# Fused attention and gated MLP on one core: one decoded weight part, two operands and the last product are placed elsewhere

## The chip, the cores and the metric

The kernel runs on one core of one Trainium2 chip. The metric is the device time of one execution in microseconds (us); lower is better. The engines that matter are PE (TensorE, matrix products), DVE (VectorE), ACT (ScalarE), POOL (GpSimd, adds only here) and SP (SyncE), whose queue issues nearly all DMAs in order.

## The reference

Inputs are float32, 8 batches, 12 heads, 448 positions, head size 64. The MLP weights have 768 x 2048 and 2048 x 768 elements and come as float64 words, which the kernel decodes itself.

```python
scores = scale * np.matmul(q, k.transpose(0, 1, 3, 2)) - np.log(S)
attn = 1.0 / (1.0 + np.exp(-scores))
x = np.matmul(attn, v)            # then (batch, position, 768)
h = x @ w_in
g = h * np.clip(h + 3.0, 0.0, 6.0) / 6.0
out = g @ w_out
```

## The kernel before, in words

**Numbers.** Each operand of the MLP is split into a high and a low part of type fp32r, and a product takes three passes (high x high, high x low, low x high). An operand therefore costs a cast on ACT or DVE and a subtraction on DVE ("put", L238 to L242, for x; `split_w`, L271, for weights; `split_2`, L394, for the second layer).

**Seven products instead of eight.** Both MLP layers are cut into 2 x 2 blocks and use a seven-product scheme; the products are called P1, P5, P6, P2, P7, P3, P4 in the order in which they run. For x the four blocks are two batches by two halves of the heads; the sums of blocks are made by `minus` and `put`. P7 and P3 use the blocks b12 and b22 ("late" in `t_ops`, L259).

**Stages.** There are four runs of attention, over batches (0,1,2,3), (4), (5,6) and (7), called runs 0 to 3, and after each a first-layer product for one pair of batches, called products 0 to 3 (`quads`). The names carry the number n. After product 3 come four blocks of the second layer (`block`, n = 0 to 3), and then the program ends. The "third pair" of batches is n = 2: its attention is run 2 (batches 5 and 6; batch 4 was done in run 1) and its product is product 2. The last single-batch run is run 3.

**A first-layer product** has four rounds jj = 0 to 3. A round makes two hidden parts i = 0, 1, and each of its 7 x 2 products has 9 matmuls, so a round has 126 matmuls and a product stage 504. Within a round, the accumulator z[P1] collects P1, P6, P7 and P4. `seed2` (L321, DVE) reads z[P1] into another bank before P7 may add to it, so **P7 waits for L321**. `h22` (L325, DVE, tile snh) reads z[P1] before P4 may add to it. Both sit in DVE's queue among the splits of weights (L275), the gates (L338), the differences (L343) and whatever else is put there.

**Decoded parts.** `prep` (L101 to L161) decodes one of eight parts of a weight matrix. A part has two halves u = 0, 1. Each half has one load (L108, SP), one ACT operation (L118), five DVE operations (L123, L125, L127, L131, L133, called "a set" below) and one POOL add (L137). Then come four POOL sums (L146) and seven stores to DRAM (L151, SP). The eight parts of w_out are placed from run 0's end to product 2; the last three, j = 5, 6, 7, all lie in product 2.

**The second layer.** For each n and each product k, eight units u of 9 matmuls: three output chunks e (banks y, y, yb) by three passes. `split_2` makes weights and g for two units at a time, with four buffers each, so all eight units of one product fit exactly. `keep`, `middle` and `out` (L422 to L446) empty the banks; `out` on P4 is an ACT multiplication (L443) and a store per chunk.

**What sets the order.** The whole program is a list of pairs (place, function). `at(place, f)` adds one; the list is sorted by place, an estimated time in us, and is emitted in that order on PE, ACT, DVE and POOL. SP's order is worked out separately from estimated readiness. An instruction waits only for data and for the one ahead of it on its engine, so a place decides who stands behind whom. In the places, TU is 1.863 us (nine matmuls), `marks[n]` is the start of product n, `starts[n]` that of run n, and `free` is the end of product n - 1.

Of the kernel before, what the change touches and what calls it, by code (L numbers as in the profile page):

```python
# [17 lines left out]
P = 128  # L18
# [5 lines left out]
NT = B // 2  # L24
# [19 lines left out]
def tile_kernel(ctx: ExitStack, tc: tile.TileContext, qk, vP, w8, outT):  # L44
# [358 lines left out]
    def block(n, place):  # L403
        z, sn = {}, {}

        def unit(k, u):
            if u == 0:
                if k in (P6, P7, P4):
                    z[k] = z[P1]
                else:  # L410
                    t = pair_banks(f"y_{n}_{k}", n + (k != P1))
                    z[k] = [t[:, 0], t[:, 1], bank(f"yb_{n}_{k}", 2 * (n % 2) + (k != P1))]
            w, x = ring.pop((n, k, u)), x2.pop((n, k, u))
            for e in range(HC):
                for i, (wu, xu) in enumerate(passes):
                    nc.tensor.matmul(  # L416
                        z[k][e][:, :S], w[:, wu, e * P : (e + 1) * P], x[:, xu],
                        start=u == 0 and i == 0 and k in (P1, P5, P2, P3), stop=u == HF - 1 and i == 2,
                        skip_group_check=True,
                    )  # L420

        def keep(k):  # L422
            for e in range(HC):
                t = two["b"].tile([P, S], F32, tag=f"sn{k}{e}", name=f"sn2_{n}_{k}_{e}")
                nc.scalar.mul(t, z[k][e][:, :S], sixth)
                sn[k, e] = t

        def plus(dst, k, e, s):
            nc.vector.scalar_tensor_tensor(
                out=dst, in0=z[k][e][:, :S], scalar=sixth, in1=sn[s, e], op0=ALU.mult, op1=ALU.add  # L430
            )

        def middle():
            for e in range(HC):
                t = two["b"].tile([P, S], F32, tag=f"c12{e}", name=f"c12_{n}_{e}")
                plus(t, P6, e, P5)
                sn["c12", e] = t

        def out(k, s, eh, th):
            for e in range(HC):  # L440
                o = two["b"].tile([P, S], F32, tag="o", name=f"o_{n}_{k}_{e}", bufs=4)
                if s is None:
                    nc.scalar.mul(o, z[k][e][:, :S], sixth)  # L443
                else:
                    plus(o, k, e, s)
                nc.sync.dma_start(out=outT[2 * n + th, e + eh * HC], in_=o)  # L446

        d = HF * TU
        for k in range(NW):
            at(place + k * d - 26, load_g, n, k)  # L450
            if n == 0:
                at(place + k * d - 24, load_w2, k)
            for u in range(HF):
                at(place + k * d + u * TU, unit, k, u)
                if u % 2 == 0:
                    at(place + k * d + u * TU - 6 * TU + 0.3, split_2, n, k, u)
        e = 0.3
        at(place + 1 * d + e, keep, P1)
        at(place + 2 * d + e, keep, P5)
        at(place + 3 * d + e, middle)  # L460
        at(place + 4 * d + e, out, P2, P1, 0, 0)
        at(place + 5 * d + e, out, P7, P5, 1, 1)
        at(place + 6 * d + e, out, P3, "c12", 0, 1)
        at(place + 7 * d + e, out, P4, None, 1, 0)

# [32 lines left out]
    for c in range(HC):  # L500
        for n in range(NT):
            own = [taken[2 * n + (h % 2), c + HC * (h // 2)] for h in range(4)]
            free = marks[n - 1] + HF * q if n else 0.0
            start = marks[n]
            if n == 0:
                early = ((own[0], dve), (own[2], dve))
                upper, both, gap = (max(own[1], own[0] + 1.2), dve), own[3] + 0.1, 1.4
                late = ((own[3] + 11, dve), (own[3] + 12.5, dve))
            elif n == 1:
                early = ((free - 11.6 * TU + 2.2 * c, act), (free - 0.5 + 9 * c, dve))  # L510
                upper, both, gap = (free - 9.6 * TU + 3 * c, act), free + 0.7 + 9 * c, 1.2
                late = ((start - 5 + 1.3 * c, dve), (start + 2 * TU + 1.5 * c, act))
            else:
                early = ((free - 11.6 * TU + 2.2 * c, act), (free - 5.6 * TU + 2.2 * c, act))
                upper, both, gap = (own[1] + 0.1, dve), own[3] + 0.1, 1.2 if n < 3 or c < 2 else 0.1
                if n == 2:
                    late = ((start - 30 + 10 * c, dve), (start - 25 + 10 * c, dve))
                else:
                    late = ((start + 4 * TU + 1.5 * c, act), (start + 6 * TU + 1.5 * c, act))
            t_ops(n, c, early, upper, both, late, gap)  # L520
    for j in range(HF):
        prep(0, j, (8, 26, 44, 74, 92, 110, 128, 146)[j], 9)
    for j, place in enumerate((
        marks[0] + 40, marks[1] + 18, marks[1] + 50, starts[2] + 26, starts[2] + 45, marks[2] + 14, marks[2] + 42, marks[2] + 68
    )):
        prep(1, j, place, 12)
    at(marks[3] + 6, open_two)
    at(now + 5.5, close_one)
    first = now
    at(now - 0.01, open_four, "psy")  # L530
# [55 lines left out]
```

## Time and profile before

| | us |
|---|---|
| three timed runs | 1118.78, 1115.82, 1117.30 (median 1117.30) |
| the profiled execution's own time | 1117.07 |
| its span, first to last instruction | 1115.2 |
| outside the span | 1.87 |
| mean granted PE clock | 0.992 |

A row of the timeline gives the start and the length in us, the engine, the line, the operation, output and input tiles, and the number of instructions merged into the row; in brackets stands how long the engine sat idle before it and who released it. Matmuls overlap: their spacing is the length of a merged row divided by its count, not the length of one. The busy length of a DVE row also overlaps the next one a little, so costs are read from start to start.

### The profile page before, as it was taken

What the parts mean: (1) busy time and instruction counts of PE and PEld (TensorE: products, weight loads), DVE (VectorE), ACT (ScalarE), POOL (GpSimd) and SP (SyncE); (2) the same over time, 40 slices, a digit from 0 to 9 for tenths busy, and PEclk for the clock granted to TensorE, in tenths of its full rate; (3) what the DMA queues carried; (4) which work ended last, traced back from release to release, by engine and by line L of the source; (5) the groups of instructions that cost most, each with busy time, mean ns of one, the idle gap of its engine ahead of it and who ended that gap; (6) DMA issues with size and microseconds to landing.
All of it is one profiled execution on the core that took longest, in us unless ns stands there. A gap on an engine that the chain in (4) does not pass through costs nothing.

```text
span 1115.2 us, 17907 instructions
## 1 busy us (share of the span) xinstructions
PE 1087.1 (97%) x6720; PEld 880.5 (79%) x6720; DVE 816.8 (73%) x1101; ACT 622.2 (56%) x841; POOL 149.1 (13%) x102
## 2 busy tenths in 40 slices
PE   8999998999999999999899999999999999999998
PEld 3447697974998743898756889999999999999997
DVE  4898799997699869799958577766655655665663
ACT  7878845457554678544467354554554455445542
POOL 1524533200033003233300000000000000000000
PEclk9999999999999999999899999999999999999999
DMA  7997998965598746899743984674533553454341
GB/s 248 294 327 231 332 336 277 338 243 169 167 318 294 278 135 211 299 309 316 243 163 99 379 301 162 263 332 157 199 132 133 182 182 132 134 173 175 110 143 60
DMA packets 95271, 250.23 MB, mean 224 GB/s; under 512 B 10576, under 2 KB 66256, under 8 KB 90704
## 3 DMA queue, kind: packets, MB, share of 16 engines
q1 hardware_dynamic: 95040, 249.01, 64.9%
q8 instruction: 53, 0.87, 0.3%
q14 instruction: 34, 0.28, 0.1%
q10 hardware_dynamic: 144, 0.07, 0.0%
HBM read 164.63 MB, written 84.41 MB: 223 GB/s over the span
## 4 chain that ended last, share of the span: by engine, by line
PE 73%; DVE 10%; DMA 8%; issue 5%; POOL 2%; ACT 2%; SPq 0%; ACTq 0%; DVEq 0%; POOLq 0%
PE y L416 24%; PE z L305 20%; PE yb L416 12%; PE sc L198 7%; PE pv L224 7%; DMA raw<-wd 2%; DVE w L275 2%; DMA gr<-gd 2%; POOL ws L146 1%; PE sc L193 1%; DVE t L343 1%; DMA st<-wi 1%; PE pv L218 1%; DVE g L338 1%; POOL wa L137 1%
## 5 line engine op out<-in xcount | busy, mean ns | idle before, releaser
L305 PE MATMUL z<-x,w 128*128 128x448 f32 x2016 | 420.5, 371 | 14.8 <-DVE z L321 12.8
L305 PEld LDWEIGHTS z<-x,w 128*128 128x128 f32 x2016 | 383.7, 191 | 52.9 <-issue 11.4
L416 PE MATMUL y<-x,w 128*128 128x448 f32 x1344 | 307.9, 364 | 0.0
L416 PEld LDWEIGHTS y<-x,w 128*128 128x128 f32 x1344 | 252.0, 187 | 19.9
L275 DVE TENSOR_TENSOR w<-w,w 128x768 fp32r<-128x768 f32 x112 | 107.3, 958 | 147.4 <-ACT w L274 146.3
L204 ACT ACTIVATE a<-sc,bias_s 128x896 f32<-128x896 f32 x168 | 168.4, 1009 | 52.4 <-PE sc L198 37.1
L274 ACT CAST w<-w 128x768 fp32r<-128x768 f32 x112 | 93.8, 838 | 184.6 <-PE yb L416 180.9
L416 PE MATMUL yb<-x,w 128*128 128x448 f32 x672 | 171.9, 364 | 0.0
L275 DVE TENSOR_TENSOR w<-raw,w 128x768 fp32r<-128x768 f32 x112 | 124.8, 1116 | 43.9 <-ACT w L274 40.2
L198 PE MATMUL sc<-qk 64*64 64x448 f32 x1152 | 149.5, 544 | 5.5 <-DMA qk<-qk 3.7
L224 PE MATMUL pv<-a,v 64*64 64x448 f32 x1152 | 149.6, 537 | 3.5 <-DVE xr L233 1.3
L416 PEld LDWEIGHTS yb<-x,w 128*128 128x128 f32 x672 | 126.0, 187 | 9.9
L399 DVE TENSOR_TENSOR x<-gr,x 128x896 fp32r<-128x896 f32 x112 | 121.6, 1086 | 6.5 <-ACT x L398 6.5
L137 POOL TENSOR_TENSOR wa<-wa,st 128x768 f32<-128x768 f32 x32 | 64.6, 2017 | 403.2 <-DVE st L133 328.7
L274 ACT CAST w<-raw 128x768 fp32r<-128x768 f32 x112 | 93.2, 832 | 38.3 <-PE z L305 17.0
L398 ACT CAST x<-gr 128x896 fp32r<-128x896 f32 x112 | 104.9, 937 | 6.5 <-DMA gr<-gd 6.5
L198 PEld LDWEIGHTS sc<-qk 64*64 64x64 f32 x1152 | 53.5, 134 | 66.0 <-issue 43.4
L224 PEld LDWEIGHTS pv<-a,v 64*64 64x64 f32 x1152 | 54.3, 133 | 61.7 <-issue 47.2
L335 ACT ACTIVATE g<-z,bias 128x448 f32<-128x448 f32 x96 | 59.8, 633 | 75.9 <-PE z L305 43.0
L335 ACT ACTIVATE g<-snh,bias 128x448 f32<-128x448 f32 x32 | 21.5, 671 | 78.1 <-DVE snh L325 75.1
L338 DVE SCALAR_TENSOR_TENSOR g<-g,z 128x448 f32<-128x448 f32 x96 | 58.4, 613 | 6.6 <-ACT g L335 6.6
L241 DVE TENSOR_TENSOR x<-xr,x 128x448 fp32r<-128x448 f32 x84 | 56.8, 678 | 8.5 <-ACT x L240 6.4
(43 smaller groups left out, 679.0 us busy)
## 6 DMA issues: line engine op xcount, KB each, us to landing
gr<-gd SPq DMA_DIRECT2D x28, 1792.0 KB, 8.2
raw<-wd SPq DMA_DIRECT2D x112, 384.0 KB, 4.8
gd<-t SPq DMA_DIRECT2D x128, 224.0 KB, 4.0
gd<-g SPq DMA_DIRECT2D x96, 224.0 KB, 3.9
qk<-qk SPq DMA_DIRECT2D x47, 448.0 KB, 5.7
st<-wi SPq DMA_DIRECT2D x16, 768.0 KB, 5.5
wd<-ws SPq DMA_DIRECT2D x64, 192.0 KB, 5.2
st<-wo SPq DMA_DIRECT2D x16, 768.0 KB, 5.6
```

The costliest lines, as they stand in the source:

```text
L137: nc.gpsimd.tensor_tensor(out=a, in0=a, in1=e, op=ALU.add)
L198: nc.tensor.matmul(sc[halves[h], j, :S], k[halves[j], ks], q[halves[j]], start=True, stop=True)
L204: nc.scalar.activation(a, sc[:, :, :S], AF.Sigmoid, bias=bias_s, scale=scale)
L224: nc.tensor.matmul(pv[b, hp][h][halves[j], :S], v[halves[h], j * NC + c], a[halves[h], j], start=c == 0 and not (second and shared), stop= ...
L274: nc.scalar.copy(h, src)
L275: nc.vector.tensor_tensor(out=l, in0=src, in1=h.bitcast(F32), op=ALU.subtract)
L305: nc.tensor.matmul(z[i, k][:, :S], w[:, wu, c * P : (c + 1) * P], X[n, k, c][:, xu], start=m == 0 and k in (P1, P5), stop=m == 3 * HC - 1, ...
L335: nc.scalar.activation(new(i, o), src(i, o), AF.Relu, bias=bias_3, scale=1.0)
L338: nc.vector.scalar_tensor_tensor(out=g[i, o], in0=g[i, o], scalar=6.0, in1=src(i, o), op0=ALU.min, op1=ALU.mult)
L398: nc.scalar.copy(x[:, 0], src)
L399: nc.vector.tensor_tensor(out=x[:, 1], in0=src, in1=x[:, 0].bitcast(F32), op=ALU.subtract)
L416: nc.tensor.matmul(z[k][e][:, :S], w[:, wu, e * P : (e + 1) * P], x[:, xu], start=u == 0 and i == 0 and k in (P1, P5, P2, P3), stop=u == H ...
```

## The change

1. **Last decoded part.** The eighth part of w_out (j = 7) moves from `marks[2] + 68`, in product 2, to `starts[3] + 1`, in run 3. The parts j = 5 and 6 stay in product 2, but move from +14 and +42 to +20 and +56. The pool of the attention (`open_two` closes it) is released at `marks[3] + 20` instead of + 6.
2. **Third pair's last two operands.** The operands of P7 and P3 of n = 2 were made before product 2, in run 2, with the casts on DVE. They are now made inside product 2 with the casts on ACT, as those of n = 3 already were.
3. **Last partial product.** The last P4 (n = 3) ran unit by unit, each over the three output chunks. It now runs chunk by chunk (`column`), each over the eight units, and each chunk is emptied when it is done.
4. In the second layer the last split of each product is placed 1 us earlier.

```diff
+        def column(k, e):
+            if e == 0:
+                z[k] = z[P1]
+            for u in range(HF):
+                w, x = ring[n, k, u], x2[n, k, u]
+                for i, (wu, xu) in enumerate(passes):
+                    nc.tensor.matmul(
+                        z[k][e][:, :S], w[:, wu, e * P : (e + 1) * P], x[:, xu],
+                        start=False, stop=u == HF - 1 and i == 2, skip_group_check=True,
+                    )
...
-        def out(k, s, eh, th):
-            for e in range(HC):
+        def out(k, s, eh, th, es=range(HC)):
+            for e in es:
...
-                at(place + k * d + u * TU, unit, k, u)
+                if (n, k) != (NT - 1, P4):
+                    at(place + k * d + u * TU, unit, k, u)
                 if u % 2 == 0:
-                    at(place + k * d + u * TU - 6 * TU + 0.3, split_2, n, k, u)
+                    at(place + k * d + u * TU - 6 * TU + 0.3 - (u == HF - 2), split_2, n, k, u)
...
-        at(place + 7 * d + e, out, P4, None, 1, 0)
+        if n < NT - 1:
+            at(place + 7 * d + e, out, P4, None, 1, 0)
+        else:
+            for h in range(HC):
+                at(place + (6 + h / HC) * d + 0.01, column, P4, h)
+                at(place + (6 + (h + 1) / HC) * d + e, out, P4, None, 1, 0, (h,))
...
-                if n == 2:
-                    late = ((start - 30 + 10 * c, dve), (start - 25 + 10 * c, dve))
-                else:
-                    late = ((start + 4 * TU + 1.5 * c, act), (start + 6 * TU + 1.5 * c, act))
+                late = ((start + 4 * TU + 1.5 * c, act), (start + 6 * TU + 1.5 * c, act))
...
-        marks[0] + 40, marks[1] + 18, marks[1] + 50, starts[2] + 26, starts[2] + 45, marks[2] + 14, marks[2] + 42, marks[2] + 68
+        marks[0] + 40, marks[1] + 18, marks[1] + 50, starts[2] + 26, starts[2] + 45, marks[2] + 20, marks[2] + 56, starts[3] + 1
...
-    at(marks[3] + 6, open_two)
+    at(marks[3] + 20, open_two)
```

**First place: DVE in the last round of product 2, ahead of the seed that its P7 waits for.** `wa_7` and `st_7_1` are the second half of part j = 7, `w_6_4` and `w_6_5` are weight splits, `x_0_0` to `x_0_2` are subtractions for the next pair, and `z_3_5_0` is the seed. Before:

```order
L343 TENSOR_TENSOR t_2_2_1_5461<-g_2_2_1_5449,t_2_2_1_5429 128x448
L123 TENSOR_SCALAR wa_7_5324<-wa_7_5324 128x768
L125 TENSOR_SCALAR wa_7_5324<-wa_7_5324 128x768
L241 TENSOR_TENSOR x_0_0_5491<-xr_0_4386,x_0_0_5491 128x448
L275 TENSOR_TENSOR w_6_4_5494<-raw_3_4_5365,w_6_4_5494 128x768
L127 SCALAR_TENSOR_TENSOR wa_7_5324<-st_7_1_5363,wa_7_5324 128x768
L241 TENSOR_TENSOR x_0_1_5510<-xr_1_4513,x_0_1_5510 128x448
L131 TENSOR_SCALAR st_7_1_5363<-wa_7_5324 128x768
L133 SCALAR_TENSOR_TENSOR st_7_1_5363<-st_7_1_5363 128x768
L275 TENSOR_TENSOR w_6_5_5526<-raw_3_5_5405,w_6_5_5526 128x768
L241 TENSOR_TENSOR x_0_2_5529<-xr_2_4629,x_0_2_5529 128x448
L321 TENSOR_TENSOR z_3_5_0_5541<-z_3_0_0_5439,sne_3_0_5508 128x448
```

After the change, the same place on DVE:

```order
L343 TENSOR_TENSOR t_2_2_1_5442<-g_2_2_1_5425,t_2_2_1_5405 128x448
L241 TENSOR_TENSOR x_0_0_5472<-xr_0_4380,x_0_0_5472 128x448
L275 TENSOR_TENSOR w_6_4_5475<-raw_3_4_5341,w_6_4_5475 128x768
L241 TENSOR_TENSOR x_0_1_5490<-xr_1_4501,x_0_1_5490 128x448
L275 TENSOR_TENSOR w_6_5_5508<-raw_3_5_5381,w_6_5_5508 128x768
L241 TENSOR_TENSOR x_0_2_5511<-xr_2_4611,x_0_2_5511 128x448
L321 TENSOR_TENSOR z_3_5_0_5523<-z_3_0_0_5415,sne_3_0_5488 128x448
```

The five decode operations ahead of this seed are gone. From the second round's seed to the third's, ten decode operations stood before and seven stand now; from the third's to the fourth's, ten before and six now.

**Second place: DVE at the start of run 3.** `xr_0` is the first attention result that is taken from its bank, `x_1_0` the operand made from it. Before, the take follows the last difference of product 2 directly:

```order
L343 TENSOR_TENSOR t_2_3_1_5731<-g_2_3_1_5711,t_2_3_1_5692 128x448
L233 TENSOR_TENSOR xr_0_5787<-pv_0_1_5740,xr_0_5787 128x448
L245 TENSOR_TENSOR xr_0_4386<-xr_0_5787,xr_0_4386 128x448
L240 CAST x_1_0_5806<-xr_0_4386 128x448
L241 TENSOR_TENSOR x_1_0_5806<-xr_0_4386,x_1_0_5806 128x448
L233 TENSOR_TENSOR xr_3_5833<-pv_3_1_5779,xr_3_5833 128x448
```

After, on DVE at the same place:

```order
L343 TENSOR_TENSOR t_2_3_1_5704<-g_2_3_1_5682,t_2_3_1_5663 128x448
L123 TENSOR_SCALAR wa_7_5693<-wa_7_5693 128x768
L125 TENSOR_SCALAR wa_7_5693<-wa_7_5693 128x768
L127 SCALAR_TENSOR_TENSOR wa_7_5693<-st_7_0_5592,wa_7_5693 128x768
L131 TENSOR_SCALAR st_7_0_5592<-wa_7_5693 128x768
L133 SCALAR_TENSOR_TENSOR st_7_0_5592<-st_7_0_5592 128x768
L233 TENSOR_TENSOR xr_0_5767<-pv_0_1_5714,xr_0_5767 128x448
L245 TENSOR_TENSOR xr_0_4380<-xr_0_5767,xr_0_4380 128x448
L240 CAST x_1_0_5787<-xr_0_4380 128x448
L241 TENSOR_TENSOR x_1_0_5787<-xr_0_4380,x_1_0_5787 128x448
L233 TENSOR_TENSOR xr_3_5814<-pv_3_1_5758,xr_3_5814 128x448
L123 TENSOR_SCALAR wa_7_5693<-wa_7_5693 128x768
```

The first half's set stands ahead of the first take; the second half's set is spread over the operations from the second take to the third.

**Third place: PE in the last product of the program.** `x_3_6_0` to `x_3_6_6` and `w_6_0` to `w_6_6` are g and weights, two units to a tile. Before, the last rows are:

```order
L416 MATMUL y_0_9273<-x_3_6_4_9900,w_6_4_9897 128x448 x6
L416 MATMUL yb_0_9274<-x_3_6_4_9900,w_6_4_9897 128x448 x3
L416 MATMUL y_0_9273<-x_3_6_6_9924,w_6_6_9921 128x448 x6
L416 MATMUL yb_0_9274<-x_3_6_6_9924,w_6_6_9921 128x448 x3
L416 MATMUL y_0_9273<-x_3_6_6_9924,w_6_6_9921 128x448 x6
L416 MATMUL yb_0_9274<-x_3_6_6_9924,w_6_6_9921 128x448 x3
```

After, PE's last ten rows are:

```order
L428 MATMUL y_0_9279<-x_3_6_4_9900,w_6_4_9897 128x448 x6
L428 MATMUL y_0_9279<-x_3_6_6_9915,w_6_6_9912 128x448 x6
L428 MATMUL y_0_9279<-x_3_6_0_9852,w_6_0_9849 128x448 x6
L428 MATMUL y_0_9279<-x_3_6_2_9876,w_6_2_9873 128x448 x6
L428 MATMUL y_0_9279<-x_3_6_4_9900,w_6_4_9897 128x448 x6
L428 MATMUL y_0_9279<-x_3_6_6_9915,w_6_6_9912 128x448 x6
L428 MATMUL yb_0_9280<-x_3_6_0_9852,w_6_0_9849 128x448 x6
L428 MATMUL yb_0_9280<-x_3_6_2_9876,w_6_2_9873 128x448 x6
L428 MATMUL yb_0_9280<-x_3_6_4_9900,w_6_4_9897 128x448 x6
L428 MATMUL yb_0_9280<-x_3_6_6_9915,w_6_6_9912 128x448 x6
```

The last tile of weights and g, `w_6_6` and `x_3_6_6`, is now needed after 18 matmuls instead of after 54, and only the chunk yb is still open when PE ends.

## The prediction

> **What bounds the kernel now.** First the page: busy time, and the slices of the span.
>
> ```profile
> span 1115.2 us, 17907 instructions
> PE 1087.1 (97%) x6720; PEld 880.5 (79%) x6720; DVE 816.8 (73%) x1101; ACT 622.2 (56%) x841; POOL 149.1 (13%) x102
> ...
> DVE  4898799997699869799958577766655655665663
> ...
> PEclk9999999999999999999899999999999999999999
> ```
>
> PE is busy for 97% of the span, so an edit can only win what PE waits (some 28 us) and what it computes at a reduced clock. The PEclk row has one 8, in slice 20 (530 to 558 us), and DVE is at 9 there. Next, who PE waits for, and the two stages that the change touches.
>
> ```profile
> PE z L305 <- DVE z L321: 12.8, 5, 4.7
> ...
> 449.60:564.70 115.10, 108.39 (x508) 97.87 (x505) 103.25 (x139) 53.64 (x85) 37.36 (x23) 0.96 0.84 284
> 565.00:597.50 32.50, 31.88 (x336) 12.35 (x328) 19.96 (x36) 25.33 (x30) 0.00 (x0) 1.00 0.36 118
> ```
>
> The largest wait is for the seed L321, 12.8 us in five waits. Product 2 (449.6 to 564.7) has DVE busy for 103.25 of 115.1 us and a clock of 0.96; run 3 has DVE busy for 19.96 of 32.5 and POOL idle. So DVE is the bound in product 2, and has room in run 3. PE's timeline gives the single losses.
>
> ```profile
> 276.87 65.94 PE L305 MATMUL z<-x,w 128*128 128x448 f32 x324
> ...
> 440.74 0.60 PE L224 MATMUL pv<-a,v 64*64 64x448 f32 x3 [1.06 <-DVE xr L233]
> ...
> 518.96 27.34 PE L305 MATMUL z<-x,w 128*128 128x448 f32 x126 [1.97 <-DVE z L321]
> 551.01 13.76 PE L305 MATMUL z<-x,w 128*128 128x448 f32 x54 [4.72 <-DVE z L321]
> 564.70 1.74 PE L198 MATMUL sc<-qk 64*64 64x448 f32 x16
> ...
> 640.01 7.53 PE L305 MATMUL z<-x,w 128*128 128x448 f32 x36 [2.10 <-DVE z L321]
> ```
>
> Undisturbed, product 1 runs at 65.94 / 324 = 0.2035 us a matmul. After the stall of 1.97 us, 126 matmuls took 27.34 instead of 25.64: 1.70 lost. After that of 4.72, 54 took 13.69 (to 564.70) instead of 10.99: 2.70 lost. After 2.10 us at 640, 36 took 7.53 against 7.33: nothing. The windows say what the loss is (the third number from the end is the granted clock).
>
> ```profile
> 519.00:522.00 3.00, 3.00 (x9) 2.65 (x10) 3.00 (x5) 0.65 (x1) 2.84 (x3) 0.51 0.94 298
> ...
> 552.00:555.00 3.00, 3.00 (x10) 2.69 (x9) 3.00 (x5) 0.00 (x0) 3.00 (x3) 0.50 0.52 112
> ```
>
> A stall can thus cost its own length and then about 1.7 us at half clock. Product 2 loses 1.97 + 1.70 + 4.72 + 2.70 = **11.1 us**.
>
> [...] Without the 1.7 the sum below would be 1107.2.
>
> **The seeds of product 2, counted on DVE.** Here are the seeds of rounds 1, 2 and 3, one decode set between them, and what POOL does to DVE.
>
> ```profile
> 489.11 1.16 DVE L321 TENSOR_TENSOR z<-z,sne 128x448 f32<-128x448 f32 x2
> ...
> 504.40 2.29 DVE L343 TENSOR_TENSOR t<-g,g 128x448 f32<-128x448 f32 x1
> ...
> 512.86 0.55 DVE L123 TENSOR_SCALAR wa<-wa 128x768 f32<-128x768 f32 x1
> 513.45 0.56 DVE L125 TENSOR_SCALAR wa<-wa 128x768 int32<-128x768 int32 x1
> ...
> 514.79 0.95 DVE L127 SCALAR_TENSOR_TENSOR wa<-st,wa 128x768 int32<-128x768 int32 x1
> 515.85 0.56 DVE L131 TENSOR_SCALAR st<-wa 128x768 int32<-128x768 int32 x1
> 516.44 0.96 DVE L133 SCALAR_TENSOR_TENSOR st<-st 128x768 f32<-128x768 uint32 x1
> ...
> 518.19 1.15 DVE L321 TENSOR_TENSOR z<-z,sne 128x448 f32<-128x448 f32 x2
> 519.25 1.54 DVE L275 TENSOR_TENSOR w<-raw,w 128x768 fp32r<-128x768 f32 x1
> ...
> 521.78 1.78 DVE L275 TENSOR_TENSOR w<-raw,w 128x768 fp32r<-128x768 f32 x1
> 523.48 1.37 DVE L123 TENSOR_SCALAR wa<-wa 128x768 f32<-128x768 f32 x1
> ...
> 548.07 2.25 DVE L241 TENSOR_TENSOR x<-xr,x 128x448 fp32r<-128x448 f32 x1
> 550.25 1.15 DVE L321 TENSOR_TENSOR z<-z,sne 128x448 f32<-128x448 f32 x2
> ```
> ```profile
> 547.37 2.47 POOL L137 TENSOR_TENSOR wa<-wa,st 128x768 f32<-128x768 f32 x1 [12.16 <-DVE st L133]
> ```
>
> A set is 0.55 + 0.56 + 0.95 + 0.56 + 0.96 = 3.58 us. The subtraction at 548.07 took 2.25 us while POOL added; an operation of its shape takes 0.62 undisturbed (the row at 573.89 further down), so the add cost 1.6. The difference at 504.40 lost as much, 1.7. A part's four sums cost DVE (519.25 to 523.48, against 0.96 for a split and 0.55 for L123) 0.6 + 0.8 + 0.8 = 2.2.
>
> - *Seed 1 to 2*: 29.08 us before. Ten decode operations (7.16) become seven (L127, L131, L133, then L123 to L131: 5.09), −2.1. One POOL add leaves, −1.7. Decode operations that lay in a wait for ACT leave too, and the wait shows: product 1, without them, has 1.47 there (row below). Between 0 and 1.5, I take +0.9. Sum 26.2.
> - *Seed 2 to 3*: 32.06 before. Ten become six (L133 and a set, 4.54), −2.6; one add leaves, −1.6. The sums now fall among differences, between 0 and 1.4 more; +0.5. Sum 28.3.
> - Seed 1 itself: part 5 moves 6 us later, so more of it lies ahead of this seed; between 0 and 1, +0.5.
>
> ```profile
> 327.54 0.96 DVE L275 TENSOR_TENSOR w<-raw,w 128x768 fp32r<-128x768 f32 x1 [1.47 <-ACT w L274]
> ```
>
> Seed 3 then starts at 489.11 + 0.5 + 26.2 + 28.3 = 544.1 and is there at 544.7. PE wants it at 516.99 (where the first stall began) + 25.64 = 542.6. So about **2.1 us of waiting remain**, between 0.2 and 4.1 by the ends above, and a half-clock stretch of 1.7 (0 to 2.7). Product 2 loses 3.8 (0.2 to 6.8) instead of 11.1: **−7.3** (−10.9 to −4.3).
>
> **The operands of P7 and P3.** They leave run 2, where twelve DVE operations go, among them some ahead of the take that PE waited for at 440.74: **−1.06** (0 to −1.06). What is next there is ACT's sigmoid, which PE follows already. In product 2 come six casts on ACT and six subtractions on DVE.
>
> ```profile
> L240 ACT CAST x<-xr 128x448 fp32r<-128x448 f32 x27 | 15.0, 567 | 4.6 <-DVE xr L245 4.6
> ```
>
> That is 6 x 0.57 = 3.4 us of ACT, busy 53.64 of 115.1 there, and as much of DVE in round 0, which has no stall; 0. If that cover were gone, P7 of round 0 would wait for up to those 3.4 us.
>
> **The moved part in run 3** brings DVE 7.2 us, two ACT operations, two loads, seven stores, and POOL six operations of 37.36 / 23 = 1.6 us, 9.7 in all.
>
> ```profile
> 573.89 0.62 DVE L233 TENSOR_TENSOR xr<-pv,xr 128x448 f32<-128x448 f32 x1 [5.83 <-ACT xr L232]
> ```
> ```profile
> 590.21 21.04 SPq L268 DMA_DIRECT2D raw<-wd  x7
> ```
>
> The first set fits into the wait of 5.83 us. The rest takes DVE to 19.96 + 7.2 + 5.4 (two adds at 1.6, the sums at 2.2) = 32.6 of 32.5 us: full, but the takes have several steps before their bank is needed. If POOL blocked DVE for all its 9.7 us, DVE would end 4.3 late. Between 0 and 4.3, I take **+0.5**, near the first, since the wait row shows so much room. On SP, loads for the last two head pairs stand behind a store that waits for POOL's first add, and the weight loads (590.21 before) behind stores that wait for its last sum, near 595. The seven loads were spread over 21 us by their buffers anyway; 0. The later release of the pool moves nothing on SP; 0. The earlier splits in the second layer meet a PE that doesn't wait; 0.
>
> **The end.**
>
> ```profile
> 1110.36 0.77 PE L416 MATMUL yb<-x,w 128*128 128x448 f32 x3
> 1110.55 0.98 ACT L443 ACTIVATE o<-y 128x448 f32<-128x448 f32 x2 [12.28 <-PE y L416]
> 1111.42 0.55 ACT L443 ACTIVATE o<-yb 128x448 f32<-128x448 f32 x1
> ```
> ```profile
> 1111.12 1.31 SPq L446 DMA_DIRECT2D outT<-o  x3
> ```
>
> PE ends at 1111.13, the third multiplication starts at 1111.42 behind two others, and three stores go out together. Alone it starts at about 1111.2, and one store is left: −0.3 (0 to −1.0). Against it stands the tile needed after 18 matmuls, 3.7 us after its buffers come free.
>
> ```profile
> L399 DVE TENSOR_TENSOR x<-gr,x 128x896 fp32r<-128x896 f32 x112 | 121.6, 1086 | 6.5 <-ACT x L398 6.5
> ...
> L398 ACT CAST x<-gr 128x896 fp32r<-128x896 f32 x112 | 104.9, 937 | 6.5 <-DMA gr<-gd 6.5
> L274 ACT CAST w<-w 128x768 fp32r<-128x768 f32 x112 | 93.8, 838 | 184.6 <-PE yb L416 180.9
> ```
>
> It takes 0.84 + 0.94 + 1.09 = 2.9 us. That fits; if it didn't, up to 1 us would be added. I take **−0.3**.
>
> **The sum.** Against the profiled execution's own 1117.07 (span 1115.2, 1.87 around it; 0.2 under the median of 1117.3): 1117.07 − 7.3 − 1.06 + 0.5 − 0.3 = **1108.9**.
>
> **Rivals.**
>
> - *All of it goes* (18%): the seed's lateness is at its low end and no half-clock stretch follows: 1117.07 − 10.9 − 1.06 + 0.2 = 1105.3. For it: product 1, also with two parts, has only one such stall. Against: in DVE's order, product 1 has six and five decode operations between these seeds; here seven and six stay.
> - *The stall only moves* (18%): seed 3 is 4.1 us late, with 2.7 at half clock, and run 2's gain is spent in run 3: 1117.07 − 4.3 + 0.2 = 1113.0, up to 1116. For it: DVE's spacing of seeds (26.2 and 28.3) is above PE's 25.64 by my own count.
> - *Slower* (7%): POOL blocks DVE for its whole length. From seed 1 to seed 3 stand eleven POOL operations, 17.8 us; I count 3 x 1.6 + 2 x 2.2 = 9.2. The other 8.6 would make seed 3 10.7 late, with 2.7 at half clock 13.4 against 11.1; run 3 adds 4.3 and 1.7. 1117.07 + 2.3 − 1.06 + 6.0 − 0.3 = 1124.0. It decides once product 2 and run 3 together lose over 8.2 us more than I count. Against: the rows above price an add of 2.47 at 1.6 and four sums at 2.2.
>
> [...]
>
> **How the numbers follow.** Forecast 57% (1106.5 to 1112), the rivals 18, 18 and 7. The unknown costs reach from 1104 to 1118; 1104.5 to 1114.5 leaves out some 13% above and 4% below. A measurement tells 0.3%, 3.35 us, from no change: faster means below 1113.9. That holds for the forecast, the first rival and a good third of the second: 82%; same 13%, slower 5%.
>
> **What would show it.** In the changed kernel, product 2 should last about 108 us instead of 115.1, with one wait for L321 of about 2 us, in round 3; no wait of 1 us on a take in run 2; run 3 within 0.5 us of 32.5; the waits at 640 as they were; and ACT's last multiplication directly behind PE. I am wrong if h22 or a seed of round 1 becomes late, if run 3 shows waits for takes, or if the last product waits for its fourth tile.

## The result, and the profile after

| | before | after |
|---|---|---|
| timed runs beside each other, median | 1116.56 us (1114.95 to 1118.78) | 1107.97 us (1105.68 to 1110.08) |
| ratio, 95% interval | | 0.9925 [0.9908, 0.9942] |
| the profiled execution's own time | 1117.07 | 1108.67 |
| run 2 (from PE's timeline) | 66.39 | 64.65 |
| product 2 | 115.07 | 106.21 |
| run 3 | 32.81 | 33.03 |
| product 3 | 105.77 | 107.64 |
| PE's last matmul to the span's end | 4.07 | 3.55 |

The change is worth 0.75%, 8.4 us between the two profiled executions. The page of the changed kernel, the lines that answer to those shown of before:

```profile
span 1106.9 us, 17894 instructions
...
PE 1083.7 (98%) x6720; PEld 878.8 (79%) x6720; DVE 810.2 (73%) x1095; ACT 624.6 (56%) x847; POOL 147.9 (13%) x102
...
DVE  4898799996699858799989577766555665665663
...
PEclk9999999999999999999999999999999999999999
```

PE's busy time fell by only 3.4 us of the 8.3 by which the span fell; the rest was waiting. The 8 in slice 20 of the clock's row is gone. PE's waits:

```profile
PE z L305 <- DVE z L321: 7.5, 4, 3.2
...
PE z L305 <- DVE w L275: 3.0, 2, 2.1
```

The wait for the seed went from 12.8 us to 7.5, but one for a weight split (L275, `w`) grew from 1.2 to 3.0, and the longest for the seed is still 3.2. PE's timeline says where they are:

```profile
448.63 88.21 PE L305 MATMUL z<-x,w 128*128 128x448 f32 x434
538.91 16.00 PE L305 MATMUL z<-x,w 128*128 128x448 f32 x70 [2.07 <-DVE w L275]
...
587.87 40.39 PE L305 MATMUL z<-x,w 128*128 128x448 f32 x198
631.42 64.25 PE L305 MATMUL z<-x,w 128*128 128x448 f32 x306 [3.16 <-DVE z L321]
```

Product 2 (448.6 to 554.8) has one stall of 2.07 us, in its last round, for the split `w_6_3`. Product 3 (587.9 to 695.5) has one of 3.16, where before had 2.10. The windows of these stages and of the two stalls (the columns are busy time and count of PE, PEld, DVE, ACT and POOL, then the granted clock, the DMA share and GB/s):

```profile
448.60:554.80 106.20, 104.13 (x508) 95.82 (x504) 92.27 (x132) 54.62 (x89) 26.18 (x17) 0.98 0.83 286
554.80:587.90 33.10, 32.48 (x338) 12.48 (x337) 28.91 (x43) 26.90 (x32) 9.33 (x6) 1.00 0.48 161
...
540.00:543.00 3.00, 3.00 (x9) 2.65 (x9) 3.00 (x5) 0.63 (x1) 0.00 (x0) 0.51 1.06 394
631.00:634.00 3.00, 2.58 (x8) 2.33 (x9) 1.74 (x4) 1.80 (x3) 0.00 (x0) 0.61 1.05 402
```

DVE lost 11.0 us of work in product 2 and gained 9.0 in run 3. Both stalls are followed by a stretch at half clock (0.51 and 0.61). DVE's queue from the second seed on shows why `w_6_3` (537.90) is late:

```profile
487.20 0.63 DVE L321 TENSOR_TENSOR z<-z,sne 128x448 f32<-128x448 f32 x1
...
513.00 0.63 DVE L321 TENSOR_TENSOR z<-z,sne 128x448 f32<-128x448 f32 x1
...
528.22 2.28 DVE L343 TENSOR_TENSOR t<-g,g 128x448 f32<-128x448 f32 x1
...
530.96 1.24 DVE L275 TENSOR_TENSOR w<-raw,w 128x768 fp32r<-128x768 f32 x1
532.12 1.43 DVE L343 TENSOR_TENSOR t<-g,g 128x448 f32<-128x448 f32 x1
533.58 1.32 DVE L343 TENSOR_TENSOR t<-g,t 128x448 f32<-128x448 f32 x1
534.83 1.43 DVE L343 TENSOR_TENSOR t<-g,g 128x448 f32<-128x448 f32 x1
...
537.90 0.95 DVE L275 TENSOR_TENSOR w<-raw,w 128x768 fp32r<-128x768 f32 x1
...
542.65 1.16 DVE L321 TENSOR_TENSOR z<-z,sne 128x448 f32<-128x448 f32 x2
```
```profile
527.85 2.17 POOL L137 TENSOR_TENSOR wa<-wa,st 128x768 f32<-128x768 f32 x1 [11.41 <-DVE st L133]
530.10 1.28 POOL L146 TENSOR_TENSOR ws<-wa 128x384 f32<-128x384 f32 x1
...
534.38 1.40 POOL L146 TENSOR_TENSOR ws<-wa,ws 128x384 f32<-128x384 f32 x1
```

The spacings of the seeds are 25.80 and 29.65 us. Beside POOL's add, a difference took 2.28 instead of 0.62; beside its four sums (530.10 to 535.78) a split took 1.24 instead of 0.95 and three differences 1.43, 1.32 and 1.43: 0.29 + 0.81 + 0.70 + 0.81 = 2.6 us of lateness, more than the 2.07 that PE waits.

### The profile page after: what moved, and what is told of

Its sections match the earlier page's. It is cut to its first block, busy times and chain, and to the rows that moved or that the text cites. A ratio compares the mean times of both kernels' runs of the same rounds, so it can differ in the third digit from the quotient of the medians.

```text
span 1106.9 us, 17894 instructions
## 1 busy us (share of the span) xinstructions
PE 1083.7 (98%) x6720; PEld 878.8 (79%) x6720; DVE 810.2 (73%) x1095; ACT 624.6 (56%) x847; POOL 147.9 (13%) x102
## 4 chain that ended last, share of the span: by engine, by line
PE 68%; issue 16%; DMA 6%; POOL 4%; DVE 4%; ACT 2%; SPq 0%; POOLq 0%; ACTq 0%; DVEq 0%
PE y L416 24%; PE z L305 19%; PE yb L416 12%; PE sc L198 5%; PE pv L224 5%; DMA raw<-wd 3%; POOL wa L137 2%; POOL ws L146 2%; DVE w L275 1%; ACT a L204 1%; PE y L428 1%; PE sc L193 1%; DMA wd<-ws 1%; PE pv L218 1%; DVE g L338 1%
## 5 line engine op out<-in xcount | busy, mean ns | idle before, releaser
L416 PE MATMUL y<-x,w 128*128 128x448 f32 x1296 | 297.2, 364 | 0.0
L416 PEld LDWEIGHTS y<-x,w 128*128 128x128 f32 x1296 | 243.0, 187 | 19.1
L275 DVE TENSOR_TENSOR w<-w,w 128x768 fp32r<-128x768 f32 x112 | 107.2, 957 | 147.0 <-ACT w L274 145.8
L416 PE MATMUL yb<-x,w 128*128 128x448 f32 x648 | 166.0, 364 | 0.0
L275 DVE TENSOR_TENSOR w<-raw,w 128x768 fp32r<-128x768 f32 x112 | 124.4, 1113 | 45.1 <-ACT w L274 42.6
L198 PE MATMUL sc<-qk 64*64 64x448 f32 x1152 | 144.2, 544 | 5.5 <-DMA qk<-qk 3.8
L224 PE MATMUL pv<-a,v 64*64 64x448 f32 x1152 | 142.7, 537 | 3.4 <-DMA v<-vP 1.9
L416 PEld LDWEIGHTS yb<-x,w 128*128 128x128 f32 x648 | 121.5, 187 | 9.6
L274 ACT CAST w<-raw 128x768 fp32r<-128x768 f32 x112 | 93.2, 832 | 38.6 <-PE z L305 21.6
```

Of the source, the lines that this page charges most:

```text
L198: nc.tensor.matmul(sc[halves[h], j, :S], k[halves[j], ks], q[halves[j]], start=True, stop=True)
L224: nc.tensor.matmul(pv[b, hp][h][halves[j], :S], v[halves[h], j * NC + c], a[halves[h], j], start=c == 0 and not (second and shared), stop= ...
L274: nc.scalar.copy(h, src)
L275: nc.vector.tensor_tensor(out=l, in0=src, in1=h.bitcast(F32), op=ALU.subtract)
L416: nc.tensor.matmul(z[k][e][:, :S], w[:, wu, e * P : (e + 1) * P], x[:, xu], start=u == 0 and i == 0 and k in (P1, P5, P2, P3), stop=u == H ...
```

## The experiments

Stage lengths are those of each run's profiled execution. The times of before beside them were 1116.25 us (first four runs), 1116.3 (next four), 1115.31 (sums_gate and best) and 1115.71 (a single execution, beside the last two). These are the stages for all of them; the last two columns are explained under best_again.

| kernel | run 2 | product 2 | run 3 | product 3 | lost in product 2 | lost in product 3 |
|---|---|---|---|---|---|---|
| before | 66.39 | 115.07 | 32.81 | 105.77 | 11.8 | 3.6 |
| after | 64.65 | 106.21 | 33.03 | 107.64 | 4.0 | 5.4 |
| part_only | 66.39 | 106.32 | 33.01 | 108.27 | 4.0 | 5.0 |
| late_only | 64.67 | 114.47 | 32.82 | 106.22 | 10.6 | 4.1 |
| end_only | 66.37 | 114.54 | 32.81 | 105.76 | 12.0 | 2.7 |
| j7_only | 64.67 | 108.17 | 33.03 | 107.85 | 5.3 | 5.7 |
| early7 | 64.67 | 106.12 | 33.92 | 105.20 | 3.6 | 3.1 |
| spread | 64.66 | 106.19 | 33.03 | 104.26 | 2.2 | 0.1 |
| sums_late | 64.68 | 106.25 | 33.02 | 107.08 | 4.0 | 4.2 |
| all3 | 64.65 | 106.25 | 33.85 | 102.25 | 4.0 | 0.1 |
| sums_gate | 64.67 | 104.35 | 33.82 | 105.88 | 0.1 | 3.0 |
| best | 64.65 | 104.35 | 33.83 | 102.25 | 0.1 | 0.1 |
| after_again | 64.66 | 106.50 | 33.03 | 107.50 | 4.1 | 5.2 |
| best_again | 64.67 | 103.29 | 34.35 | 104.25 | 1.1 | 0.1 |

### The three parts, each alone

**part_only**: before, with the decoded parts moved.

```diff
-        ..., marks[2] + 14, marks[2] + 42, marks[2] + 68
+        ..., marks[2] + 20, marks[2] + 56, starts[3] + 1
...
-    at(marks[3] + 6, open_two)
+    at(marks[3] + 20, open_two)
```

> Of the change only the decoded parts and the pool's release are moved; the operands of P7 and P3 stay in run 2, the last product runs unit by unit. Theory (product 2 was bound by DVE, and a set and its POOL operations gone from it are the gain): product 2 lasts 105.5 to 108 us instead of 115.1, the wait for a take in run 2 stays near 1 us, the end stays at about 4.1 us behind PE's last matmul; 1109 to 1111 us. Rival (the gain comes from the operands that leave run 2): product 2 keeps a seed wait of over 3 us and lasts over 111 us; 1113 us or more.

1109.79 us, ratio 0.9941 [0.9925, 0.9958]. Product 2 falls to 106.32, as in the whole change, and product 3 rises to 108.27. Its timeline on PE:

```profile
439.36 0.60 PE L224 MATMUL pv<-a,v 64*64 64x448 f32 x3 [1.06 <-DVE xr L233]
...
538.60 16.04 PE L305 MATMUL z<-x,w 128*128 128x448 f32 x70 [2.12 <-DVE w L275]
```

The stall for `w_6_3` is there, and the take's wait in run 2 has stayed. So both what product 2 gains and what product 3 loses belong to the moved part.

**late_only**: before, with the third pair's last two operands made in its product.

```diff
-                if n == 2:
-                    late = ((start - 30 + 10 * c, dve), (start - 25 + 10 * c, dve))
-                else:
-                    late = ((start + 4 * TU + 1.5 * c, act), (start + 6 * TU + 1.5 * c, act))
+                late = ((start + 4 * TU + 1.5 * c, act), (start + 6 * TU + 1.5 * c, act))
```

> Of the change only the operands of P7 and P3 of the third pair are made in product 2; three decoded parts stay there. Theory: run 2 loses its wait of 1.06 us for a take and lasts 64.5 to 65 us instead of 66.4; product 2 stays at 114 to 117 us with waits for L321 in rounds 2 and 3; 1114 to 1117 us. Rival (DVE enters product 2 with less left over from run 2, and that is the gain): product 2 lasts under 110 us and the time falls below 1112 us.

1113.91 us, 0.9981 [0.9971, 0.9990], just below the range expected. Run 2 falls to 64.67, and the two stalls of product 2 stay (row by row on PE's timeline):

```profile
516.53 18.83 PE L305 MATMUL z<-x,w 128*128 128x448 f32 x90 [1.96 <-DVE z L321]
...
548.63 12.91 PE L305 MATMUL z<-x,w 128*128 128x448 f32 x54 [5.00 <-DVE z L321]
```

The operations that came into product 2 are hidden there, as counted.

**end_only**: before, with the last product by output chunk and the earlier last split (the diff's `column`, `out` and `split_2`).

> Of the change only the last product runs chunk by chunk and the second layer's last splits stand 1 us earlier. Theory: the span ends 3.5 to 3.7 us after PE's last matmul instead of 4.1, no wait on PE at the last product's fourth tile; 0.3 to 0.8 us faster than before, which the timed rounds can't tell from none. Rival (the fourth tile is late): a gap on PE of up to 1 us about 3.7 us into the last product, and no gain.

1115.37 us, 0.9992 [0.9982, 1.0003]: not to be told from no change. In the trace, the end itself is shorter; the last matmuls and the one multiplication behind them:

```profile
1106.46 5.02 PE L428 MATMUL yb<-x,w 128*128 128x448 f32 x24
```
```profile
1111.52 0.54 ACT L454 ACTIVATE o<-yb 128x448 f32<-128x448 f32 x1 [3.88 <-PE yb L428]
```

PE ends at 1111.48 and the span at 1115.0, 3.5 us later, against 4.07 before. The three parts together make 0.9941 x 0.9981 x 0.9992 = 0.9914, within the interval of the whole.

**j7_only**: the changed kernel, with parts 5 and 6 at +14 and +42 as before.

```diff
-        ..., marks[2] + 20, marks[2] + 56, starts[3] + 1
+        ..., marks[2] + 14, marks[2] + 42, starts[3] + 1
```

> The changed kernel, but parts 5 and 6 at +14 and +42 as before; only the last part has left product 2. Theory (what is taken away counts, the spacing of the two others little): round 2 holds both halves of part 6 ahead of its seed as before, so a wait for L321 of 0 to 2 us stays there, and round 3 has none; product 2 lasts 104 to 108 us; 1106 to 1110 us. Rival (the new spacing is the gain): waits of 2 us or more in both rounds, product 2 over 110 us; 1112 us or more.

1108.55 us, 0.9926 [0.9911, 0.9941], no other than the whole change. The stall is now that of the third round's seed:

```profile
517.71 38.93 PE L305 MATMUL z<-x,w 128*128 128x448 f32 x180 [1.97 <-DVE z L321]
```

Product 2 took 108.17 instead of 106.21 in this execution. The new spacing of parts 5 and 6 decides which instruction is late; that it saves time beyond that is not shown.

### Product 3's loss

On SP's queue, behind product 3's first gate store, stand loads for the second layer (gr and w2, L391 and L386, two of each, of 1792 and 1536 KB). In the changed kernel the first goes out 16.28 us into product 3 (604.15 - 587.87):

```profile
604.15 0.42 SPq L391 DMA_DIRECT2D gr<-gd  x1
604.62 0.43 SPq L386 DMA_DIRECT2D w<-wd  x1
...
607.42 0.71 SPq L386 DMA_DIRECT2D w<-wd  x1
```

Behind them ACT waits for weight loads (a row of its timeline), and so the seed is late:

```profile
628.91 0.83 ACT L274 CAST w<-raw 128x768 fp32r<-128x768 f32 x1 [3.65 <-DMA raw<-wd]
```

Before, the first of these loads went out 14.86 us into product 3 (612.37 - 597.51). The theory: the moved part makes the first gate late, the burst of loads starts 1.42 later, and the seed with it.

**early7**: the changed kernel with the part 9 us earlier.

```diff
-        ..., marks[2] + 56, starts[3] + 1
+        ..., marks[2] + 56, starts[3] - 8
```

> The changed kernel with the last decoded part placed 9 us earlier, at the end of product 2 (its POOL sums then lie in the middle of run 3). In the four kernels that have this part at the start of run 3, product 3 lasts 107.6 to 108.3 us, in those that don't 105.8 to 106.2, and its first store of a gate leaves 15.9 us after the product's start instead of 14.5. Theory (POOL's sums hold DVE back at the end of run 3, the first gate comes late, the large second-layer loads behind its store start late, and so does what they delay): the first store comes 14.4 to 14.8 us in, the wait for L321 is 2.2 us or less, product 3 lasts 105.5 to 106.5; 1105 to 1108 us. [...]

1106.74 us, 0.9907 [0.9880, 0.9935]; product 3 105.20. On SP the burst is back at 14.86 us (602.76 - 587.90), and the stall on PE is 2.20:

```profile
602.76 0.42 SPq L391 DMA_DIRECT2D gr<-gd  x1
```
```profile
630.50 19.80 PE L305 MATMUL z<-x,w 128*128 128x448 f32 x94 [2.20 <-DVE z L321]
```
```profile
629.50:632.50 3.00, 2.00 (x10) 1.90 (x11) 1.78 (x4) 1.26 (x2) 0.00 (x0) 1.00 1.08 389
```

No half clock follows this stall. The price is a wait of 1.16 us in run 3 for a gate, behind the part that now stands ahead of it. The median lies among the changed kernel's own times (1105.68 to 1110.08), so a gain in time is not shown.

How the part makes the first gate late can be read on DVE, since product 3 starts at 587.87 in the changed kernel and at 587.90 in early7. First rows of the changed kernel, then of early7:

```profile
577.58 1.92 DVE L240 CAST x<-xr 128x448 fp32r<-128x448 f32 x1
...
603.14 0.61 DVE L338 SCALAR_TENSOR_TENSOR g<-g,z 128x448 f32<-128x448 f32 x1
```
```profile
577.73 0.40 DVE L240 CAST x<-xr 128x448 fp32r<-128x448 f32 x1
...
596.80 0.96 DVE L275 TENSOR_TENSOR w<-raw,w 128x768 fp32r<-128x768 f32 x1 [1.31 <-ACT w L274]
...
601.75 0.61 DVE L338 SCALAR_TENSOR_TENSOR g<-g,z 128x448 f32<-128x448 f32 x1
```

In the changed kernel POOL's last add and its four sums (577.09 to 584.72) lie beside DVE's last operands of run 3. Five DVE operations there take 3.8 us more, from start to start, than the same ones in early7, where POOL has ended by 574.93. DVE then has no wait up to the first gate, at 603.14. In early7 it waits for ACT twice (0.83 and 1.31 us) and takes this gate at 601.75. So DVE carries its lateness from run 3 into product 3, and the gate, its store and the first load are each 1.39 us later.

The other runs bear this out. Behind this seed PE goes on 42.46 to 42.60 us into product 3 where the first load leaves at 14.86 to 15.08 us (before, late_only, end_only, early7), and 42.79 to 44.20 us into it where the load leaves at 16.26 to 16.30 (after, after_again, part_only, j7_only, and sums_late and sums_gate below). The half clock, some 1.6 us, is not bound to the late burst: it came in five of these six runs (the granted clock fell to 0.61 in after, to 0.67 in after_again), and in late_only of the four others.

**spread**: the changed kernel with the four loads let go one at a time, each behind a one-element DVE write to its buffer.

```diff
+        if k < 2:
+            nc.vector.memset(t[:, 0, :1], 0.0)
...
+        if n == 0 and k < 2:
+            nc.vector.memset(t[:, 0, :1], 0.0)
...
-            at(place + k * d - 26, load_g, n, k)
+            begin = marks[3] + 22 + 32 * k
+            at(begin if n == 0 and k < 2 else place + k * d - 26, load_g, n, k)
...
-                at(place + k * d - 24, load_w2, k)
+                at(begin + 16 if k < 2 else place + k * d - 24, load_w2, k)
```

> The changed kernel, with the first two loads of g and of w_out for the second layer (6.6 MB) held back to four places spread over product 3, each by one element that DVE writes into the tile first. Theory (PE's wait in product 3 comes from weight loads that stand in this burst): ACT's waits for raw<-wd between 15 and 55 us into product 3 go from 3 us each to under 1, no wait for L321 over 0.7 us there, product 3 lasts 103 to 104.5 us instead of 107.6; 1103.5 to 1106 us. Rival (the loads are late by themselves, or spreading only moves the wait): a wait of 1.5 us or more remains later in product 3, which lasts 106 us or more.

1102.76 us, 0.9872 [0.9845, 0.9899], below the changed kernel's interval and 0.7 us below the range expected. SP's queue has the loads 12 to 19 us apart:

```profile
612.74 0.32 SPq L395 DMA_DIRECT2D gr<-gd  x1
...
626.52 0.32 SPq L388 DMA_DIRECT2D w<-wd  x1
...
645.89 0.33 SPq L395 DMA_DIRECT2D gr<-gd  x1
...
658.24 0.32 SPq L388 DMA_DIRECT2D w<-wd  x1
```

PE waits for nothing in product 3, in this run and in the three others that have this edit (all3, best, best_again). So the burst of loads is what makes that seed late. The moved part put it 1.42 us later. The edit also starts the loads later, 24.7 us into the product (612.74 - 588.05) instead of 16.28; whether it is this or the spacing that counts wasn't tried apart. Before has the same burst and a stall of 2.10 us for the same seed; that the burst made that one too wasn't tried, since the edit was made on the changed kernel alone.

### Product 2's remaining stall

**sums_late**: the changed kernel with part 6's four POOL sums and their stores placed 18 us later.

```diff
+        wait = 18 if (which, j) == (1, 6) else 0
...
-            at(place + gap + 10.5 + 1.3 * i, sums, i)
+            at(place + gap + 10.5 + wait + 1.3 * i, sums, i)
...
-        at(place + gap + 17, store, "s", (P5, P6, P7, P3))
+        at(place + gap + 17 + wait, store, "s", (P5, P6, P7, P3))
```

> The changed kernel, with the four POOL sums and the last stores of part 6 placed 18 us later, behind the last round's seed; the adds stay. Theory (the wait of 2.07 us for the split w_6_3 in product 2 is DVE's lateness from these sums): the differences at that place take 0.62 us instead of 1.3 to 1.4, PE has no wait over 0.7 us in product 2, which lasts 103 to 104 us instead of 106.2; 1104.5 to 1107 us. Rival (DVE is late there by its own work): a wait of 1.5 us or more remains in round 3 and product 2 lasts 105.5 us or more.

1107.35 us, 0.9912 [0.9888, 0.9936]. The edit missed its aim, as POOL's timeline shows:

```profile
525.30 2.18 POOL L137 TENSOR_TENSOR wa<-wa,st 128x768 f32<-128x768 f32 x1 [11.41 <-DVE st L133]
527.56 1.28 POOL L146 TENSOR_TENSOR ws<-wa 128x384 f32<-128x384 f32 x1
```

A place sets the order on an engine, not a time, and POOL has nothing between. The stall (2.09 us) stayed, and the question was open.

**all3**: early7, sums_late and spread together.

> The changed kernel with all three: the last part 9 us earlier, part 6's sums 18 us later, and the four large loads spread. Theory: the gains lie in different stages and add up: product 2 103 to 104 us, product 3 103 to 104.5; 1100 to 1103.5 us. Rival (they share DVE, and one gives back what another wins): product 2 and 3 together over 209 us; 1105 us or more.

1102.83 us, 0.9870 [0.9851, 0.9890]; the same as spread. Product 2 stayed at 106.25, where 103 to 104 was expected, since this kernel's edit for it is that of sums_late. Once the loads go singly, the earlier place of the part gains nothing that shows.

**sums_gate**: the changed kernel with the sums really held: DVE writes one element of their tile behind the last round's splits.

```diff
+        def hold():
+            wt["s"] = att.tile([P, 4, W], F32, tag="ws", name=f"ws_{which}_{j}")
+            nc.vector.memset(wt["s"][:, 0, :1], 0.0)
...
+        wait = 15.5 if (which, j) == (1, 6) else 0
+        if wait:
+            at(place + gap + 10.4 + wait, hold)
...
-            at(place + gap + 10.5 + 1.3 * i, sums, i)
+            at(place + gap + 10.5 + wait + 1.3 * i, sums, i)
```

> The changed kernel, but POOL's four sums of the moved part (part 6 of the second weight) are really held back: DVE writes one element of their tile behind the last round's last split in product 2, and the sums, which overwrite that element, and their four stores come behind it. Placing them later in the code alone had left them where they were, since POOL has nothing else to do there. Theory A (the wait of 2.07 us for split w_6_3 in product 2 of the changed kernel is DVE's lateness by POOL's sums, which stretch about five DVE instructions by 0.3 to 0.8 us each, 2.6 us together; and the half clock behind that wait costs about 1.2 more): the sums begin at about 545 us instead of 530, no wait of over 0.7 us is left in product 2, product 2 takes 102.5 to 104 us instead of 106.2, the time is 1104 to 1107 us (product 0 may differ by 2 us either way between executions). Theory B (the split is late by POOL's add alone or by DVE's own order, the sums only lie beside it): the wait stays at 1.5 us or more and product 2 at 105.5 to 106.5. Theory C (the lateness only moves: the sums now stretch the last splits and the first casts of run 3): the wait for w_6_3 goes, but one of over 1 us shows at the end of product 2 or at the start of run 3, and product 2 and run 3 together gain less than 1.5 us.

1106.21 us, 0.9916 [0.9898, 0.9934]. POOL's and DVE's timelines:

```profile
528.02 2.18 POOL L137 TENSOR_TENSOR wa<-wa,st 128x768 f32<-128x768 f32 x1 [11.41 <-DVE st L133]
543.70 1.02 POOL L150 TENSOR_TENSOR ws<-wa 128x384 f32<-128x384 f32 x1 [13.51 <-DVE ws L141]
```
```profile
528.39 2.29 DVE L350 TENSOR_TENSOR t<-g,g 128x448 f32<-128x448 f32 x1
...
532.65 0.62 DVE L350 TENSOR_TENSOR t<-g,t 128x448 f32<-128x448 f32 x1
...
535.45 0.95 DVE L282 TENSOR_TENSOR w<-raw,w 128x768 fp32r<-128x768 f32 x1
```

With the sums gone from there, the differences take 0.62 us, the split starts at 535.45, and product 2 has no stall: theory A for the wait. Its length of 104.35 lies above what A said (102.5 to 104); the next section says why. Part of it does move, as theory C said: run 3 begins with a wait for a gate on PE,

```profile
554.67 2.06 PE L205 MATMUL sc<-qk 64*64 64x448 f32 x16 [0.84 <-DVE g L345]
```

and takes 0.8 us longer. Product 2 and run 3 together gain 1.1 us in this execution; by the medians the gain over the changed kernel isn't outside the intervals.

**best**: spread and sums_gate together.

> The changed kernel with both repairs: the sums of the moved part held back as in the run beside it, and the four large second-layer loads of product 3 let go one at a time by a one-element DVE write each. If the two repairs are independent (theory A of the run beside it, and the burst of loads as the cause of product 3's wait): product 2 takes 102.5 to 104 us, product 3 102 to 104.5, no wait of over 0.7 us in either, and the time is 1098 to 1102 us, against 1102.8 us with the loads let go singly alone. If the lateness by the sums only moves, or product 2's loss returns as another wait: 1102 to 1105 us.

1101.01 us (1100.40 to 1101.70), 0.9867 [0.9848, 0.9886]: below before and below the changed kernel (0.9867 / 0.9925 = 0.994 of it). Against spread alone (0.9872) the difference is not shown. Neither product 2 nor product 3 has a stall.

### One execution more, for the pace

In best, two products without a stall and with a clock of 1.00 differ by 2 us. PE's groups in a window around product 2, then around product 3:

```profile
L312 PE MATMUL z<-x,w 128*128 128x448 f32 x504 | 104.4, 368 | 0.0
...
L312 PE MATMUL z<-x,w 128*128 128x448 f32 x504 | 102.4, 365 | 0.0
```

The starts of the matmuls in the trace are 206.7 ns apart in the one and 202.7 in the other, from the first to the last: 504 x 4 ns = 2.0 us. Two runs without edits asked whether the program sets this.

**after_again**: the changed kernel, unaltered.

> The changed kernel once more, unaltered, for a second profiled execution. In the profiles so far the 504 matmuls of a product that never stalls take either 102.4 or 104.4 us at full clock (their starts 202.7 or 206.7 ns apart), and the pace changes from product to product and at stalls. Theory A (the pace is a matter of the execution, not of the program): the four products of this execution show another pattern of the two paces than those of the first profile (product 0 slow for some 70% of its length, products 1, 2 and 3 nearly all fast), and the products' lengths differ by up to 2 us each, while the waits stay: about 2.1 us for split w_6_3 in product 2 and 3 to 3.8 us for a seed in product 3. Theory B (the pace is set by the program's order): the same pattern within 0.3 us for each product.

**best_again**: the kernel best, unaltered.

> The kernel with both repairs once more, unaltered. Theory A (the pace is a matter of the execution): products 2 and 3, which have no stall, each take either about 102.3 or about 104.3 us or a mixture, not bound to 104.35 and 102.25 as in the first profile. Theory B (the program sets it): 104.3 for product 2 and 102.3 for product 3 again. In both, no wait of over 0.7 us in product 2 or 3, and a time of 1099 to 1102 us.

1106.82 and 1102.07 us, one execution each. In after_again, product 1 is the one with the slow pace (by 1.6 us of its length, against 0.2 in the first profile), and product 0 took 106.72 instead of 108.85; in best_again, product 2 ran at 202.7 and product 3 at 206.7 ns, the reverse of best. So the pace belongs to the execution, not to the program. The waits came back: 2.09 us for `w_6_3` and 2.72 for the seed in after_again. In best_again, with a fast product 2, waits of 0.71 us for the last seed and 1.37 for the gate in run 3 show: DVE is still the bound there, by a hair. The wait for `w_6_3` stays away in this fast product too, so its absence in sums_gate is not owed to the slow pace of product 2 there.

The two columns "lost" in the table take the pace off: the length, less 504 x 0.2027 = 102.2 us, less the excess of all spacings under 0.25 us over 0.2027. What is left is stalls and half clock. They also show that product 2 took 106.1 to 106.5 us with a fast pace and 4.0 lost (after) as with a slow one and 2.2 lost (spread): where DVE sets the end, a slower PE only waits less.

## Why the prediction was right, and where it was not

The time forecast was 1108.9 us; 1107.97 was measured, and the profiled executions differ by 8.4 us where 8.2 was forecast. By step:

| step | forecast | profiled |
|---|---|---|
| product 2 | -7.3 | -8.86 |
| run 2 | -1.06 | -1.74 |
| run 3 | +0.5 | +0.22 |
| the end | -0.3 | -0.52 |
| product 3 | 0 | +1.87 |
| product 0, product 1, the rest | 0 | +1.13, -0.33, -0.2 |

- **Product 2: right in mechanism and size.** The remaining loss was to be 3.8 us, a stall of 2.1 and a half clock; it was 4.0, a stall of 2.07 and a half clock. That the bound is DVE's queue, and that the moved part frees it, part_only shows (product 2 takes 106.32 us instead of 115.07). The half clock came, as the row with 0.51 shows. The 1.7 for it, between 0 and 2.7, stands on the three stalls of before: 1.70 after 1.97 us, 2.70 after 4.72, nothing after 2.10. That a stall of about 2 us can go either way the runs bear out: a wait of 2.07 us was charged here, and one of 2.20 in early7 was not. What decides it no run shows.
- **The place of the stall: one step off.** It was put at the last round's seed; it fell on the split seven rows ahead of it in DVE's queue, `w_6_3`, since the sums that stretch DVE lie just before. The spacings of 25.80 and 29.65 were forecast as 26.2 and 28.3; their sum is 0.95 higher; the first seed came 38.6 us into the product (487.20 - 448.63), 1.4 earlier than counted. sums_gate shows the cause: with the sums away from there, PE has no wait in product 2. The price taken for the sums, 2.2 + 0.5 = 2.7, was right: they cost 2.6. What was off is whose wait it lengthens.
- **Product 2's extra 1.5 us.** 1.1 of it is the pace of before's own product 2, known only from the later traces; about 0.7 are short losses of before (11.8 against the 11.1 counted from three rows).
- **Run 2: the wait was undersized.** Its row says 1.06 us of idle time, but a row's idle time begins at the modelled end of the last matmul. The row ahead of it on before's timeline,

```profile
438.77 0.91 PE L224 MATMUL pv<-a,v 64*64 64x448 f32 x2
```

  has two matmuls from 438.77 to 440.74, where eight take 0.75 us: 1.97 - 0.19 = 1.78 lost, and 1.74 came back. late_only shows that it is this edit.
- **Run 3: right for the stage itself.** Run 3 grew by 0.22, and the rival that POOL blocks DVE for its whole length is out: beside the 7.6 us of POOL from 577.09 to 584.72 DVE lost 3.8. Single operations fared differently: beside POOL's add of 2.17 us (527.85) a difference took 2.28 instead of 0.62, but a gate at 530.42, beside POOL's first sum of 1.28, took 0.61, as the one at 525.62 did with POOL idle. What DVE lost was not made up by the end of run 3, though; it reached PE one stage later.
- **The end: right in sign**, 0.5 instead of 0.3, in end_only too.
- **Product 3: the step that failed.** Two terms were wrong. DVE's lateness by the moved part was charged to run 3 alone (+0.5), though DVE was counted as full there; it went on into product 3 and made the first gate 1.42 us late. And SP was priced at 0, since the weight loads are spread by their buffers; what was not followed is the next thing on SP, a gate store with 6656 KB of second-layer loads behind it. The cost was 1.8 us (5.4 lost instead of 3.6): a stall 1.06 longer and a half clock that before did not have, less a wait of 0.75 us for h22 that only before had. early7 moves the gate and the burst back, and spread removes the stall. Of the prediction's own signs, "the waits at 640 as they were" failed for this reason. The half clock's share is partly chance: in this product it came after a wait of 2.18 us in late_only, and not after 1.60 in sums_gate or 2.20 in early7.
- **Product 0** has the same instructions in both kernels; the +1.13 is the pace (1.5 us of its length in after, none in before). It is chance, and so is the pace's share in product 2.

That the sum came within 1 us of the median is in part luck, for misses of opposite signs cancel: -1.6 in product 2 and -0.7 in run 2 against +1.9 in product 3 and +1.1 in product 0.

## What to carry to other kernels

When work is moved out of a stage, follow the queues at its new place one stage further than the work itself: here the cost sat not in the stage that took the work but in the burst of loads behind the first store after it. Placing POOL's sums later changed nothing here, since POOL had nothing to do before them (sums_late); a dependence did (sums_gate). A one-element write from the engine that should go first is a cheap one, for a POOL operation (0.06 us on DVE in sums_gate) as for a large load (spread). Price a stall on PE from start to start, not by the idle column, and compare stages over several executions before a difference of 2 us is given a cause.

## What the runs showed of the hardware that was not expected

- The same 504 matmuls took 102.4 or 104.4 us at a granted clock of 1.00 and without idle time: starts 202.7 ns apart in product 3 of best, 206.7 in its product 2. Each pace held there over the whole product, and best_again has the two the other way round. The pace also changes within a product: product 1 of after_again ran at 206.7 ns up to 340 us and at 202.6 from 360 on, with a wait of 1.23 us for a seed at 344. The second layer's matmuls have one pace, 202.2 ns, in before, after, sums_gate, all3, best, after_again and best_again. What sets it stays open.
- A half-clock stretch came behind some stalls of 1.6 to 3.2 us and not behind others. It came after 1.97 (j7_only: the 180 matmuls behind it took 38.93 us, against 36.5 to 37.2 at the two paces), 2.07 (after, clock 0.51), 2.72 (after_again, 0.67) and 3.16 (after, 0.61). It did not come after 1.60 (sums_gate, 1.00), 1.96 (late_only, the same seed as in j7_only: the 90 matmuls behind it took 18.83 us, against 18.6 at the slow pace) and 2.20 (early7, 1.00).
- Letting four loads of 6656 KB in all go 12 to 19 us apart and later, instead of within 4 us, removed a stall of 3 us and its half clock from the changed kernel.
